# Fourier attention and gated MLP on one Trainium2 core: engine orders and PSUM banks from a list schedule of recorded instructions

## The chip, the core and the metric

The kernel runs on one core of one Trainium2 chip. The metric is device microseconds for one execution. Five engines have queues of their own and work strictly in the order of their queue: TensorE (PE in the rows; its weight loads are PEld), VectorE (DVE), ScalarE (ACT), GpSimd (POOL) and SyncE (SP, which here only issues DMAs). An engine waits for another at a semaphore, and everything behind the waiting instruction in its queue waits too.

## What is computed

Four batches of 1088 tokens with 128 features go through three stages, each in fp32:

```python
q_p, k_p = phi(q), phi(k)                  # products of two 8-wide projections, per head
x = (q_p @ kv) / (q_p @ z)                 # linear attention, kv = k_p^T v, z = sum of k_p
u = x + real(fft(fft(x, axis=1), axis=2))  # Fourier mixing over tokens and features
x2 = u + relu(norm(u) @ w_ch1) @ w_ch2     # channel MLP
h = relu(x2 @ w_in); gate, v = h[..., :512], h[..., 512:]
v_s = einsum('ts,bsd->btd', w_spatial, norm(v)) + b_spatial
out = (gate * v_s) @ w_out
```

The weights of the MLPs arrive as float64 and are turned into float32 on the chip. A wide fp32 product is made of fp32r products: each operand is split into a high and a low part, and three matmuls (high by high, high by low, low by high) are summed in PSUM.

## The kernel before, in words

Per batch there are four parts. **keys and queries** (`feats`, `keys`, `queries`): small matmuls into the tile `abp`, copied by ScalarE to `ab`, multiplied out by VectorE to `pp` (128x768); then `kv`, transposes `qps`, `nm`, and VectorE's division into `ub`. **Fourier** (`fourier_seq`, `fourier_feat`): VectorE folds `ub` (`eo`, `fe`, `l_`, `lrb`), TensorE makes `dft`, ScalarE copies it to `tb`, TensorE makes `ups` and `urm`, and VectorE adds them to `ub`. **channel**: statistics (`bst`, `mv`) and normalisation `un` of nine 128-token tiles, transposes `t1` and `t2`, then for each of three groups c of 384, 384 and 320 tokens the MLP in four blocks m: three matmuls into `h_`, ScalarE's relu `hh`, VectorE's remainder `hl`, three matmuls into `c2`. The sum goes to `xt` and is split into `xh` and `xl`; per 128 tokens `v_ps` is made, relu `v`, statistics, normalisation; and v is split into `vh` (ScalarE) and `vlo`. **spatial**: for each group c and each of four feature blocks m, 24 matmuls of `vh`, `vlo` with the spatial weights `wsh`, `wsl` and two for the remaining tokens and bias go into one accumulator `ac`; `u_ps` gives the gate, `uh` and `gl`/`gh` the gated product, `o` the output. Its matmuls of 384 or 320 columns are the bulk of TensorE's work: lines 608 to 610 have 1152 of them over the four batches.

There is one `vh`/`vlo` pair, so a batch's spatial part can begin only when its v is ready and the batch before is through with it. The spatial weights come in raw (`wst`, `w2st`) and are split too, in `spatial_split`: ScalarE makes `wsh`, VectorE or GpSimd `wsl`. The raw tiles of groups 0 and 1 share their buffers with `uh`, `gh`, `gl`, `sxh` and `sxl` of the spatial part (`ring`).

The order is set in three ways. The text of the kernel gives an order; the tile framework's scheduler may move instructions within it, by its own cost estimates; and some places are pinned by hand: `tc.keep_in_program_order` on the idle matmuls `wp` of `warm` and on `dft`, `tc.issue_after` on the first spatial weights. Batch b+1's `channel` and batch b's `spatial` are Python generators that the last loop (lines 640 to 654) advances by turns at the ratio `R`. Matmuls `wp` on zeros (`warm`, 11, 10 and 20 of them) are there to keep TensorE active. PSUM's eight banks are split between two pools, `psx` and `psy`, with fixed tags: `x` 3, `y` 1, `acc` 2, `us` 1, `o` 1.

Lines that the change touches: 195 (`un` on VectorE, a subtraction and a multiplication by per-partition scalars), 202 and 206, 271 (`vlo` of batch 0 on GpSimd, `sub(G, ...)`), the generators' `yield`s, `spatial` (588 to 638) and the loops behind 562.

Of the kernel before, what the change touches and what calls it, by code (L numbers as in the profile page):

```python
# [1 line left out]

# [5 lines left out]
F32 = mybir.dt.float32  # L8
# [55 lines left out]

@with_exitstack
def fourier_attention_gmlp_kernel(
# [18 lines left out]
    nc = tc.nc  # L85
    V, A, T, G = nc.vector, nc.scalar, nc.tensor, nc.gpsimd
# [23 lines left out]
    ub, x2, marks = {}, {}, {}  # L110
# [6 lines left out]
    def spatial_load(pool, c, stage):  # L117
# [47 lines left out]
    def channel(b, pe, psm, tagm, nm, psc, tagc, vn, hooks=(None,) * 7):  # L165
# [9 lines left out]
        def stats(tiles):  # L175
# [5 lines left out]
            r_ = rstd(pe, mv_, len(tiles), "l1", nb)  # L181
            for i, j in enumerate(tiles):
                mv[j], rs[j] = mv_[:, i, 0:1], r_[:, i, :]
# [6 lines left out]
        for c in range(3):  # L190
# [3 lines left out]
            for j, i in tiles:  # L194
                marks[b, c, "un"] = V.tensor_scalar(out=un[:, i, :], in0=u_[:, j, :], scalar1=mv[j], scalar2=rs[j],
                                op0=ALU.subtract, op1=ALU.mult)
            t1 = mt("t1")
            for j, i in tiles:
                marks[b, c, "t1"] = T.transpose(out=t1[:, 128 * i:128 * i + 128], in_=un[:, i, :], identity=ident if j < 8 else psel)
            unh = pe.tile([P, 384], F32R, tag="unh", bufs=nb, name="unh")  # L200
            unl = pe.tile([P, 384], F32R, tag="unl", bufs=nb, name="unl")
            marks[b, c, "unh"] = A.copy(out=unh[:, 0:n], in_=t1[:, 0:n])
# [6 lines left out]
            yield  # L209
# [32 lines left out]
            marks[b, c] = A.copy(out=xh[:, 0:n], in_=xt[:, 0:n])  # L242
# [8 lines left out]
            for j, i in tiles:  # L251
# [11 lines left out]
                yield  # L263
# [23 lines left out]
    sa = ExitStack()  # L287
    ca = sa.enter_context(tc.tile_pool(name="ca", bufs=1, side="right"))
    sp = ExitStack()
    pre = sp.enter_context(tc.tile_pool(name="pre", bufs=1, side="left"))  # L290
# [34 lines left out]
    def weight_load(tag, *blocks):  # L325
        t = const.tile([P, len(blocks), 512], I32, tag=tag, name="wraw")
        for i, (n, src, k) in enumerate(blocks):
            nc.sync.dma_start(out=t[:, i, :], in_=src.bitcast(I32)[:, 512 * k:512 * k + 512])
# [100 lines left out]
    def fourier_seq(b):  # L429
# [34 lines left out]
        def dft(par, sine, lhsT, rhs, last):  # L464
            c0 = 64 * (sine ^ par)
            m_ = mm(out=dps[par][c0:c0 + 64, 0:NCOL], lhsT=lhsT, rhs=rhs, start=(par, sine) not in done, stop=last,  # L466
                    tile_position=(0, c0))
            if done:
                tc.keep_in_program_order(m_)
# [50 lines left out]
    def warm(n):  # L520
        wp = psy.tile([P, 512], F32, tag="us", bufs=1, name="wp")
        for i in range(n):
            tc.keep_in_program_order(mm(out=wp, lhsT=wz[:, 0:128], rhs=wz, start=True, stop=True))
# [3 lines left out]
    nc.sync.dma_start(out=raw0, in_=sblk.bitcast(I32))  # L527
# [13 lines left out]
    nc.sync.dma_start(out=tr, in_=trig)  # L541
    nc.sync.dma_start(out=trr, in_=trig_r)
    nc.sync.dma_start(out=dd, in_=ddft)
# [18 lines left out]
    for _ in channel(0, pre, psy, "acc", 2, psy, "o", None, [convert(("w2", 0), ("w2", 1), ("wo", 0), ("wo", 1)), None, None, None, convert(("wi", 0), ("wi", 1)), None]):  # L562
        pass
# [3 lines left out]
    with tc.issue_after(marks[0, 1, "t1"].ins):  # L567
        spatial_split(pre, 0, [G], spatial_load(const, 0, ring))
# [186 lines left out]
```

## Time and profile before

| what | us |
|---|---|
| median of 3 runs | 455.65 (455.12 to 455.97) |
| span of the profiled execution, first to last instruction | 451.9 |
| median less that span | 3.75 |
| busy: TensorE, VectorE, ScalarE, GpSimd | 430.6, 276.3, 191.5, 67.1 |
| first matmul of the spatial part (`ac`) | at 73.30 |

The profiled execution has a span of its own and no separate time; the 3.75 us between it and the median lie before the first and behind the last instruction, or are the difference of the runs. Busy time is the union of an engine's instructions; a matmul overlaps the next one, so TensorE's pace is read from the distance of two starts, not from one matmul's length. Idle time of an engine is put down to the instruction of another engine that ended last before it went on.

### The profile page before, as it was taken

How to read it: one execution, taken by the hardware profiler on the slowest of the kernel's cores; microseconds unless marked ns; L12 is line 12 of the kernel's file. 1: busy time of each engine (PE TensorE's matmuls, PEld its weight loads, DVE VectorE, ACT ScalarE, POOL GpSimd, SP SyncE). 2: the span in 40 equal slices, each digit the busy share in tenths (PEclk: the TensorE clock that was granted, in tenths of full speed). 3: DMA queues.
4: the chain of work that ended last, by engine and by line, in shares of the span. 5: the costliest groups of instructions: out<-in, count | busy, mean ns of one | idle time of the engine just before them, and what ended most of it. 6: DMA issues, size and time to landing. Idle time of an engine off the chain costs nothing.

```text
span 451.9 us, 8066 instructions
## 1 busy us (share of the span) xinstructions
PE 430.6 (95%) x3181; PEld 392.3 (87%) x3181; DVE 276.3 (61%) x685; ACT 191.5 (42%) x448; POOL 67.1 (15%) x105
## 2 busy tenths in 40 slices
PE   8786999999999989999999999999999999999996
PEld 7555877768787878899999999999999999999995
DVE  5899898995657677788536454873727366221221
ACT  3755787455231345456424233552424255222211
POOL 2354684570111130000000000000000000000000
PEclk9999799999999999999999999999999999999998
DMA  8974151011004000000000000000000000000000
GB/s 256 363 249 159 36 167 48 1 47 27 1 1 133 19 0 0 1 20 1 16 0 1 17 1 1 19 15 1 1 1 17 1 18 1 16 0 19 0 19 15
DMA packets 13009, 19.32 MB, mean 43 GB/s; under 512 B 1446, under 2 KB 11436, under 8 KB 12844
## 3 DMA queue, kind: packets, MB, share of 16 engines
q1 hardware_dynamic: 12972, 18.82, 12.9%
q8 instruction: 25, 0.41, 0.4%
q14 instruction: 12, 0.10, 0.1%
HBM read 16.58 MB, written 2.23 MB: 42 GB/s over the span
## 4 chain that ended last, share of the span: by engine, by line
PE 73%; DVE 9%; issue 9%; ACT 4%; POOL 3%; DMA 1%; POOLq 0%; ACTq 0%; DVEq 0%
PE ac L610 12%; PE ac L608 12%; PE ac L609 12%; PE v_ps L254 2%; PE dft L466 2%; PE v_ps L256 2%; PE c L227 2%; PE c L225 2%; PE c L226 2%; PE v_ps L255 2%; PE ac L616 2%; PE ac L615 2%; PE u_ps L601 2%; PE u_ps L602 1%; PE u_ps L603 1%
## 5 line engine op out<-in xcount | busy, mean ns | idle before, releaser
L608 PE MATMUL ac<-wsh,vh 128*128 128x384 f32 (+1 forms) x384 | 126.6, 330 | 0.4 <-ACT vh L270 0.4
L610 PE MATMUL ac<-wsh,vlo 128*128 128x384 f32 (+1 forms) x384 | 126.4, 329 | 0.0
L609 PE MATMUL ac<-wsl,vh 128*128 128x384 f32 (+1 forms) x384 | 126.3, 329 | 0.0
L609 PEld LDWEIGHTS ac<-wsl,vh 128*128 128x128 f32 x384 | 72.1, 188 | 1.8 <-issue 0.8
L608 PEld LDWEIGHTS ac<-wsh,vh 128*128 128x128 f32 x384 | 72.1, 188 | 1.5 <-ACT vh L270 0.7
L610 PEld LDWEIGHTS ac<-wsh,vlo 128*128 128x128 f32 x384 | 72.1, 188 | 1.4 <-issue 0.6
L619 DVE TENSOR_TENSOR uh<-ac,uh 128x384 f32<-128x384 f32 (+1 forms) x48 | 25.5, 531 | 55.9 <-PE ac L616 55.2
L605 ACT ACTIVATE uh<-u_ps 128x384 f32<-128x384 f32 (+1 forms) x48 | 22.6, 471 | 48.0 <-PE u_ps L603 45.6
L114 DVE TENSOR_TENSOR gl<-uh,gh 128x384 fp32r<-128x384 f32 (+1 forms) x48 | 25.8, 538 | 13.5 <-ACT gh L620 13.4
L245 POOL CAST xh<-xh 128x64 fp32r<-128x64 f32 x4 | 2.0, 496 | 202.5 <-ACT xh L242 202.5
L361 DVE TENSOR_TENSOR pp<-ab 128x768 f32<-128x768 f32 x23 | 23.9, 1067 | 11.3 <-ACT ab L357 11.3
L620 ACT CAST gh<-uh 128x384 fp32r<-128x384 f32 (+1 forms) x48 | 23.6, 492 | 13.2 <-DVE uh L619 13.0
L261 DVE BATCH_NORM_STATS2 bst<-vn 128x6 f32<-128x512 f32 x27 | 18.6, 693 | 16.8 <-ACT vn L259 16.7
L259 ACT ACTIVATE vn<-v_ps 128x512 f32<-128x512 f32 x27 | 16.0, 598 | 19.2 <-PE v_ps L256 18.7
L241 DVE TENSOR_TENSOR xt<-c,xt 128x384 f32<-128x384 f32 (+1 forms) x12 | 6.4, 530 | 27.4 <-PE c L227 27.4
L227 PE MATMUL c<-hl,w 128*128 128x384 f32 (+1 forms) x48 | 16.7, 348 | 0.3 <-DVE hl L220 0.3
L282 ACT CAST vh<-vn 128x1024 fp32r<-128x1024 f32 x12 | 12.6, 1048 | 10.3 <-PE ac L609 8.1
L225 PE MATMUL c<-hh,w 128*128 128x384 f32 (+1 forms) x48 | 16.7, 348 | 0.0
L242 ACT CAST xh<-xt 128x384 fp32r<-128x384 f32 (+1 forms) x12 | 6.0, 496 | 25.0 <-DVE xt L241 24.9
L254 PE MATMUL v_ps<-wi,xh 128*128 128x512 f32 x36 | 15.5, 430 | 0.9 <-ACT v L259 0.8
L226 PE MATMUL c<-hh,w 128*128 128x384 f32 (+1 forms) x48 | 16.3, 340 | 0.0
L601 PE MATMUL u_ps<-sxh,wi 128*128 128x384 f32 (+1 forms) x48 | 16.3, 339 | 0.0
(714 smaller groups left out, 931.1 us busy)
## 6 DMA issues: line engine op xcount, KB each, us to landing
wst<-in_wsp SPq DMA_DIRECT2D x18, 192.0 KB, 4.0
vx<-in_vt SPq DMA_DIRECT2D x12, 198.0 KB, 4.0
kt<-in_kT SPq DMA_DIRECT2D x12, 192.0 KB, 3.6
qt<-in_qT SPq DMA_DIRECT2D x12, 192.0 KB, 4.5
w2st<-in_wsp SPq DMA_DIRECT2D x9, 160.0 KB, 5.6
tr<-in_trig SPq DMA_DIRECT2D x1, 1096.0 KB, 8.7
wraw<-in_w SPq DMA_DIRECT2D x4, 256.0 KB
wraw<-in_win SPq DMA_DIRECT2D x4, 256.0 KB, 6.2
```

The source lines that it names most:

```text
L114: eng.tensor_tensor(out=lo, in0=x, in1=hi.bitcast(F32), op=ALU.subtract)
L225: mm(out=c2[:, 0:n], lhsT=wpart("w2", 0, 128 * m, 128), rhs=hh[:, 0:n], start=(m == 0), stop=False)
L226: mm(out=c2[:, 0:n], lhsT=wpart("w2", 1, 128 * m, 128), rhs=hh[:, 0:n], start=False, stop=False)
L227: mm(out=c2[:, 0:n], lhsT=wpart("w2", 0, 128 * m, 128), rhs=hl[:, 0:n], start=False, stop=(m == 3))
L254: mm(out=h_, lhsT=xh[:, cs], rhs=wt["wi"][:, 2:4, 0, :], start=True, stop=False)
L361: (G if [b, tag[0], c] in [[3, 'k', 2]] else V).tensor_tensor(out=pp, in0=a_.unsqueeze(3).to_broadcast([P, 12, 8, 8]), in1=b_.unsqueeze(2) ...
L601: mm(out=h_[:, 0:n], lhsT=wpart("wi", 0, 128 * m, 128), rhs=xh[:, 0:n], start=True, stop=False)
L608: mm(out=ac[:, 0:n], lhsT=vh[:, k, ms], rhs=wsh[c][:, k, :], start=(k == 0), stop=False)
L609: mm(out=ac[:, 0:n], lhsT=vh[:, k, ms], rhs=wsl[c][:, k, :], start=False, stop=False)
L610: mm(out=ac[:, 0:n], lhsT=vl[:, k, ms], rhs=wsh[c][:, k, :], start=False, stop=False)
L619: V.tensor_tensor(out=uh[:, 0:n], in0=ac[:, 0:n], in1=uh[:, 0:n], op=ALU.mult)
L620: A.copy(out=gh[:, 0:n], in_=uh[:, 0:n])
```

## The change

The kernel no longer issues instructions as its text runs. Engines and tiles are stand-ins that record each instruction with what it reads and writes (`Plan`, `Op`, `Tile`, `View`). `price` gives each a duration by a formula. `arrange` runs a list schedule up to 12 times, alternately from the front and from the back, each time with urgencies from the last pass, and keeps the order with the least planned end; `run` then issues the instructions in that order under `tc.manual_schedule()`. PSUM has one pool of eight banks, and the schedule gives each tile a bank when its first instruction is placed. The hand-set order (`issue_after`, `keep_in_program_order`, the generators and `R`) is gone. DMAs are taken in the order of their recording as they become ready.

Two edits are in the arithmetic's place: `un` is made by ScalarE as Identity(scale * x + bias), with `sh` = -mean * rstd made by one VectorE instruction per batch; and batch 0's eight `vlo` are made by VectorE.

```diff
+class Plan:
...
+    def arrange(self):
+
+        self.edges()
+        best, urgent = None, [-r for r in self.rank]
+        for _ in range(self.rounds):
+            there = self.schedule(urgent, True)
+            if there is None:
+                break
+            ends, issued = there
+            if best is None or max(ends) < best[0]:
+                best = max(ends), issued, ends, {t: t.bank for t in self.banked}
+            back = self.schedule(ends, False)
+            if back is None:
+                break
+            urgent = [-e for e in back[0]]
...
+    def run(self):
+        self.arrange()
+        with self.tc.manual_schedule():
+            for o in self.issued:
+                o.emit()
...
+    def price(self, op):
...
+        elif e == "scalar":
+            op.busy = (160 if psum else 190) + n / 1.2
+        elif e == "vector":
+            if op.meth == "tensor_scalar" and not psum and not out.tile.pool.psum:
+                ptr = isinstance(kw.get("scalar1"), View)
+                op.busy, op.port = (260 if ptr else 145) + n / 1.92, True
...
+                        if s <= t:
+                            turn = e == "tensor" and mode is not None and o.mode != mode
+                            s = max(s, free[e] + 230 if turn else free[e], port if o.port and forth else 0.0)
+                            choice.append((sign * urgent[o.n] + (self.sticky if turn else 0.0), sign * o.n, s, o))
...
-    const = ctx.enter_context(tc.tile_pool(name="const", bufs=1, side="left"))
-    psx = ctx.enter_context(tc.tile_pool(name="psx", bufs=1, space=PSUM))
-    psy = ctx.enter_context(tc.tile_pool(name="psy", bufs=1, space=PSUM))
+    const = plan.pool("const", side="left")
+    psx = psy = plan.pool("ps", psum=True)
...
+            sh = pe.tile([P, len(tiles), 1], F32, tag="sh1", bufs=nb, name="sh")
+            V.scalar_tensor_tensor(out=sh, in0=mv_[:, :, 0:1], scalar=-1.0, in1=r_, op0=ALU.mult, op1=ALU.mult)
...
-                marks[b, c, "un"] = V.tensor_scalar(out=un[:, i, :], in0=u_[:, j, :], scalar1=mv[j], scalar2=rs[j],
-                                op0=ALU.subtract, op1=ALU.mult)
+                A.activation(out=un[:, i, :], in_=u_[:, j, :], func=ACTF.Identity, scale=rs[j], bias=mv[j])
...
-                        sub(G, vl[:, j, :], v_, vh[:, j, :])
+                        sub(V, vl[:, j, :], v_, vh[:, j, :])
...
-    with tc.issue_after(marks[0, 1, "t1"].ins):
-        spatial_split(pre, 0, [G], spatial_load(const, 0, ring))
+    spatial_split(pre, 0, [G], spatial_load(const, 0, ring))
...
     for b in range(B):
-        sg = spatial(b)
         if b + 1 < B:
-            R = [0.3, 2.2, 2.2][b]
...
+            channel(b + 1, pe, psx, "x", 3, psx, "y", vn)
+        spatial(b)
+    plan.run()
```

In the rows below `L168` is the line that issues everything in the new kernel. First, TensorE's queue around the first spatial matmul (`ac`). Before, with `c` the MLP's second product and `v_ps` the v of batch 0's last group still to come:

```order
L399 MATMUL qps<-prm,pp 128x128 x4
L227 MATMUL c_864<-hl,w_68 128x320
L399 MATMUL qps<-prm,pp 128x128 x2
L354 MATMUL abp<-sb_s,qt 64x2x32 x6
L608 MATMUL ac<-wsh_1199,vh 128x384
L609 MATMUL ac<-wsl_1200,vh 128x384
L610 MATMUL ac<-wsh_1199,vlo 128x384
L608 MATMUL ac<-wsh_1199,vh 128x384
L609 MATMUL ac<-wsl_1200,vh 128x384
L610 MATMUL ac<-wsh_1199,vlo 128x384
L254 MATMUL v_ps<-wi,xh 128x512
```

And in the new order, where the number in `kvz_73` and `kvz_65` tells odd and even batches apart:

```order
L168 MATMUL c_1342<-hh,w_1055 128x320 x2
L168 MATMUL nm<-kvz_65,qp 64x66 x7
L168 MATMUL v_ps<-wi,xl 128x512 x3
L168 MATMUL c_1342<-hl,w_1055 128x320
L168 MATMUL nm<-kvz_65,qp 64x66 x12
L168 MATMUL nm<-kvz_73,qp 64x66 x12
L168 MATMUL ac<-wsh_1463,vh 128x384 x4
L168 MATMUL ac<-wsl_1471,vh 128x384
L168 MATMUL ac<-wsh_1463,vlo 128x384
```

The first `ac` now stands behind all `v_ps` of batch 0's second group, as before, and also behind the `abp`, `kv` and most `nm` of all four batches; four accumulators are opened at once instead of one.

Second, VectorE's queue at the Fourier fold of batch 0 (`eo`, `fe`, `l_`, `lrb` are its steps, `pp` belongs to the keys and queries of batch 1). Before:

```order
L312 TENSOR_SCALAR dy<-wraw 128x256
L442 TENSOR_TENSOR eo<-ub 128x512 x2
L446 TENSOR_TENSOR fe<-eo 128x4x63
L455 TENSOR_TENSOR lrb<-rs__414 32x63
L451 TENSOR_TENSOR l__416<-fe 128x2x64 x2
L455 TENSOR_TENSOR lrb<-rs__414 32x63
L446 TENSOR_TENSOR fe<-eo 128x4x63
L455 TENSOR_TENSOR lrb<-rs__414 32x63
L451 TENSOR_TENSOR l__416<-fe 128x2x63 x2
L455 TENSOR_TENSOR lrb<-rs__414 32x63
```

And now:

```order
L168 TENSOR_TENSOR eo<-ub 128x512 x2
L168 TENSOR_TENSOR pp<-ab 128x768 x4
L168 TENSOR_TENSOR fe<-eo 128x4x63
L168 TENSOR_TENSOR l__79<-fe 128x2x63
L168 TENSOR_TENSOR pp<-ab 128x768 x2
L168 TENSOR_TENSOR fe<-eo 128x4x63
L168 TENSOR_TENSOR l__79<-fe 128x2x63
L168 TENSOR_TENSOR lrb<-rs__421 32x63 x4
```

The six `pp` of batch 1 stand between the steps of batch 0's fold where there were none.

Third, VectorE's queue in the MLP of batch 1 (`hl` is the remainder of a block m, `unl` that of the normalised input). Before, these are the first group's four blocks:

```order
L114 TENSOR_TENSOR unl<-t_1972,unh 128x384
L195 TENSOR_SCALAR un<-ub,mv_1933,r_1961 128x128 x2
L220 SCALAR_TENSOR_TENSOR hl<-h__2268,hh 128x384
L220 SCALAR_TENSOR_TENSOR hl<-h__2276,hh 128x384
L220 SCALAR_TENSOR_TENSOR hl<-h__2284,hh 128x384
L220 SCALAR_TENSOR_TENSOR hl<-h__2298,hh 128x384
L241 TENSOR_TENSOR xt<-c_2267,xt 128x384
L619 TENSOR_TENSOR uh<-ac,uh 128x384
```

And now the end of the second group's four blocks, `hl<-h__2339` being the last of them:

```order
L168 SCALAR_TENSOR_TENSOR hl<-h__2297,hh 128x384
L168 TENSOR_TENSOR xl<-xt,xh 128x384
L168 SCALAR_TENSOR_TENSOR hl<-h__2303,hh 128x384
L168 SCALAR_TENSOR_TENSOR hl<-h__2309,hh 128x384
L168 BN_STATS bst<-vn 128x6
L168 BN_AGGR mv_2351<-bst 128x2
L168 BN_STATS bst<-vn 128x6
L168 SCALAR_TENSOR_TENSOR hl<-h__2339,hh 128x384
```

The `un` between them are gone from VectorE, and everything of keys, queries and Fourier for all batches stands ahead of both pieces, in both orders.

## Rows read from the trace of the kernel before

**Rows 1.** The page: span, and busy time of the engines.
```profile
span 451.9 us, 8066 instructions
...
PE 430.6 (95%) x3181; PEld 392.3 (87%) x3181; DVE 276.3 (61%) x685; ACT 191.5 (42%) x448; POOL 67.1 (15%) x105
```

**Rows 2.** Windows: length; busy us of PE, PEld, DVE, ACT, POOL; granted clock; DMA.
```profile
0.00:73.00 73.00, 61.09 (x583) 48.67 (x585) 61.83 (x165) 45.73 (x115) 37.48 (x54) 0.95 0.60 195
73.00:171.00 98.00, 92.91 (x961) 76.76 (x958) 69.94 (x163) 40.34 (x99) 27.40 (x45) 1.00 0.10 29
0.00:171.00 171.00, 154.00 (x1538) 125.43 (x1539) 131.77 (x327) 86.07 (x213) 64.88 (x99) 0.98 0.31 100
40.00:60.00 20.00, 16.97 (x103) 14.31 (x103) 17.58 (x39) 14.94 (x37) 12.69 (x13) 0.83 0.35 108
...
60.00:100.00 40.00, 37.43 (x336) 29.15 (x338) 36.28 (x80) 24.83 (x57) 25.52 (x30) 1.00 0.20 57
200.00:440.00 240.00, 240.00 (x1438) 234.37 (x1437) 120.54 (x295) 89.19 (x199) 1.48 (x4) 1.00 0.03 9
```

**Rows 3.** Waits of VectorE from 73 to 171 us: total us, times, longest.
```profile
DVE ub L503 <- PE ups L495: 7.7, 4, 4.4
DVE pp L361 <- ACT ab L357: 7.5, 7, 2.1
DVE rd L420 <- PE nm L411: 3.7, 2, 1.8
```

**Rows 4.** TensorE in order of time: start, length, line, tiles, the idle time before.
```profile
73.30 0.44 PE L608 MATMUL ac<-wsh,vh 128*128 128x384 f32 x1
73.58 0.34 PE L609 MATMUL ac<-wsl,vh 128*128 128x384 f32 x1
73.76 0.34 PE L610 MATMUL ac<-wsh,vlo 128*128 128x384 f32 x1
...
171.51 0.34 PE L225 MATMUL c<-hh,w 128*128 128x384 f32 x1
```

**Rows 5.** The same view of TensorE at 40 to 46 us.
```profile
40.59 0.33 PE L199 MATMUL t<-prm,un 128*128 128x128 f32 x1 [1.95 <-DVE un L195]
...
43.74 0.69 PE L216 MATMUL h__641<-unl,w 128*128 128x384 f32 x1 [0.81 <-DVE unl L114]
44.23 0.52 PE L214 MATMUL h__649<-unh,w 128*128 128x384 f32 x1
44.55 0.52 PE L215 MATMUL h__649<-unh,w 128*128 128x384 f32 x1
```

**Rows 6.** VectorE by line and shape: count, busy us, mean ns, idle before.
```profile
L195 DVE TENSOR_SCALAR un<-ub,mv,r 128x128 f32<-128x128 f32 x36 | 11.4, 360 | 0.1
...
L114 DVE TENSOR_TENSOR vlo<-vn,vh 128x1024 fp32r<-128x1024 f32 x12 | 14.6, 1214 | 0.3 <-ACT vh L282 0.3
...
L261 DVE BATCH_NORM_STATS2 bst<-vn 128x6 f32<-128x512 f32 x27 | 18.6, 693 | 16.8 <-ACT vn L259 16.7
...
L114 DVE TENSOR_TENSOR xl<-xt,xh 128x384 fp32r<-128x384 f32 x8 | 4.8, 595 | 1.8 <-ACT xh L242 1.5
...
L114 DVE TENSOR_TENSOR wsl<-wst,wsh 128x384 fp32r<-128x384 f32 x4 | 5.2, 1367 | 0.0
...
L220 DVE SCALAR_TENSOR_TENSOR hl<-h__2268,hh 128x384 fp32r<-128x384 f32 x1 | 0.6, 558 | 2.2 <-ACT hh L219 2.2
```

**Rows 7.** GpSimd by line and shape.
```profile
L114 POOL TENSOR_TENSOR wsl<-wst,wsh 128x384 fp32r<-128x384 f32 x12 | 15.5, 1314 | 1.9 <-ACT wsh L134 1.7
L114 POOL TENSOR_TENSOR vlo<-v,vh 128x512 fp32r<-128x512 f32 x8 | 10.8, 1378 | 6.0 <-ACT vh L270 6.0
```

**Rows 8.** ScalarE by line and shape.
```profile
L314 ACT ACTIVATE dy<-dy,cst 128x256 int32<-128x256 int32 x10 | 5.1, 506 | 0.1
...
L311 ACT ACTIVATE dr<-wraw 128x256 f32<-128x256 uint32 x10 | 4.4, 443 | 4.4 <-POOL w L114 2.5 <-POOL wo L114 1.5 <-POOL wi L114 0.2
...
L277 ACT CAST a<-vn 128x128 fp32r<-128x128 f32 x12 | 3.5, 294 | 0.0
```

More of the change, by code (lines that the diff above doesn't have):

```diff
@@ new lines, with __init__, tile, open @@
+class Pool:
+    def __init__(self, plan, name, after=None, psum=False, **kw):
+        self.plan, self.name, self.prev, self.kw, self.psum = plan, name, after, kw, psum
+        self.tiles, self.tags, self.stack, self.handle = [], {}, None, None
+    def tile(self, shape, dtype, tag=None, bufs=1, name=None):
+        t = Tile(self, shape, dtype, tag or name, bufs, name)
+        if not self.psum:
+            self.tags.setdefault(t.tag, []).append(t)
+        self.tiles.append(t)
+        if self.psum:
+            self.plan.banked.append(t)
+        return t
+    def open(self):
+        if self.handle is None:
+            if self.prev is not None:
+                self.prev.stack.close()
+                self.plan.opened.remove(self.prev)
+            self.stack = ExitStack()
+            kw = dict(space=PSUM) if self.psum else self.kw
+            self.plan.opened.append(self)
+            self.handle = self.stack.enter_context(self.plan.tc.tile_pool(name=self.name, bufs=1, **kw))
+        return self.handle
@@ new lines, with emit, __init__, __getattr__ @@
+class Op:
+    __slots__ = ("n", "eng", "meth", "args", "kw", "pre", "busy", "lag", "mode", "port", "banked", "start", "end")
+    def emit(self):
+        if self.eng.handle is not None:
+            r = lambda v: v.real() if isinstance(v, View) else v
+            getattr(self.eng.handle, self.meth)(*[r(v) for v in self.args], **{k: r(v) for k, v in self.kw.items()})
+class Engine:
+    def __init__(self, plan, name, handle):
+        self.plan, self.name, self.handle = plan, name, handle
+    def __getattr__(self, meth):
+        def record(*args, **kw):
+            return self.plan.add(self, meth, args, kw)
+        return record
@@ L284, in conv @@
         conv_rem(ms, vn[:, 8, ms])
[L287 to L290, printed above, removed]
+    ca = plan.pool("ca", side="right")
+    pre = plan.pool("pre", side="left")
     tr = ca.tile([P, 2, 4, NCOL], F32, name="tr")
@@ L465, in dft @@
             c0 = 64 * (sine ^ par)
-            m_ = mm(out=dps[par][c0:c0 + 64, 0:NCOL], lhsT=lhsT, rhs=rhs, start=(par, sine) not in done, stop=last,
+            mm(out=dps[par][c0:c0 + 64, 0:NCOL], lhsT=lhsT, rhs=rhs, start=(par, sine) not in done, stop=last,
                     tile_position=(0, c0))
-            if done:
-                tc.keep_in_program_order(m_)
             done[par, sine] = True
@@ L566, in fourier_attention_gmlp_kernel @@
     loads(2)
[L567 to L571 removed]
+    spatial_split(pre, 0, [G], spatial_load(const, 0, ring))
+    pw = plan.pool("pw", after=pre, side="left", reuse_waits="tile")
     spatial_split(ca, 1, (V, G), spatial_load(pw, 1, ring))
@@ L580, in fourier_attention_gmlp_kernel @@
         fourier_feat(b)
-    sa.close()
-    pe = ctx.enter_context(tc.tile_pool(name="pe", bufs=1, side="right", reuse_waits="tile"))
+    pe = plan.pool("pe", after=ca, side="right", reuse_waits="tile")
     w2st = pe.tile([P, 10, CH[2][1]], F32, tag="vn", name="w2st")
@@ L589, in spatial @@
     def spatial(b):
-        pend = None
         for c in range(3):
```

350 lines of the change are left out of this document (296 added, 54 removed).

## The prediction

> **What bounds the kernel now.** I read the page first: TensorE is busy 430.6 of 451.9 us, VectorE 276.3 [rows 1]. A share of 95% says little about where time is to be had, so I went to the windows. From 200 to 440 us TensorE is busy 240.00 of 240.00 us at granted clock 1.00 [rows 2]; a matmul of 384 columns starts 0.18 us after the one before it (73.58 to 73.76) [rows 4], and no order makes that shorter. The reader is to see there that the last 280 us are TensorE at its own pace. The time to be had lies before. Of the first 171 us TensorE is idle 17.0 (171 less 154.0), and VectorE is idle 39.2: 11.2 of the first 73 us, 28.1 of the 98 behind [rows 2].
>
> The waits of VectorE say what the 28.1 are. Between 73 and 171 us it waits 7.7 us for `ups`, 7.5 for `ab` and 3.7 for `nm` [rows 3], 18.9 in all: keys, queries and Fourier of batches 1 to 3, which TensorE's queue hands out in small portions between `ac` matmuls. Nothing there is short of work; the two engines take turns.
>
> **The mark.** To compare the orders I choose a place from which TensorE has the same work left in both. Before, it is the matmul at 171.51 us [rows 4]: behind it stand 926 matmuls of 384 columns, 584 of 320, 81 of 512 and 48 of 128. In the new order, behind the third block's `c2<-hl` of batch 1's second group stand 937, 584, 75 and 42: eleven at 0.18 us more, six wider and six narrower ones less, equal to within half a us. The matmul there needs `hl`, and the last `hl` of that group (`h__2339`, the third place shown above) stands close behind, so I take that as VectorE's mark. Whatever the new order gains by the mark it keeps, as TensorE is full behind it, and the tail (last `o`, copy, DMA) is the same. So the question is one number: when is the new order at the mark?
>
> **VectorE's work ahead of the mark.** By 171 us it has been busy 131.8 us [rows 2]. The new order puts the same front work ahead of the mark, with these differences, counted over both orders:
> - `un`: 15 gone, at 0.360 us [rows 6]: -5.4.
> - `vlo` of batch 0: 8 more. VectorE has no such row. A subtraction of 1024 columns takes 1.214 and one of 384 takes 0.595 [rows 6]; on the line between them 512 columns take 0.72: +5.8. The lower end is 0.595 each (+4.8), the upper 1.367, which is what `wsl` takes on VectorE while GpSimd does its share of the same split (+10.9).
> - `hl`: 4 more at 0.558: +2.2; `bst` of v: 2 more at 0.693: +1.4 [rows 6].
> - `unl`, `xl`, `xt` one more each and `uh`, `gl` one less each, all of about 0.56: +0.6. Two `sh` and one `mv`, which are among the smallest instructions: I put +0.6 for them.
>
> Sum: +5.2, so 137.0 us of busy time.
>
> **Its idle time.** This is what the change is about, and no row shows it. Ends: the 11.2 of the first 73 us hold the wait for the first loads, which stays; if the order takes out 3 of them and no idle time is added, 8. At the other end, from 60 to 100 us, where VectorE is the fuller engine, it idles 3.7 of 40 [rows 2], that is 0.09 per us; over the some 75 us that remain that gives 7, and twice that, 14, added to 8 gives 22. I take 11.2 plus half of 7, 15 in round: the keys and queries now stand early (TensorE has all `abp` and `kv` ahead of the first `ac`, the first place shown above), and the second place shows `pp` filling the gaps of batch 0's fold. So the mark is at 137.0 + 15 = 152.0 instead of 171.5: **19.5 us less**.
>
> Can TensorE be there by then? Until 171 us it is busy 154.0 [rows 2]. In that are some 24 matmuls that follow at 0.32 us (44.23 to 44.55 [rows 5]) instead of 0.18, 3.4 us, after TensorE had waited for `unl` and before that for `un`; without them it is 150.6, and that still contains the stretched steps within it. So it allows 152 but not much less unless those steps shrink too, which is a second reason for not taking 8.
>
> **What costs nothing.** `un` on ScalarE: a copy of 128 columns is 0.294 us; two activations of 256 columns with and without a pointer bias are 0.506 and 0.443 [rows 8], so a pointer costs 0.06 and `un` with two about 0.42. 15 of them ahead of the mark are 6.3 us beside 86.1 of busy time until 171 [rows 2]: 92 of 152, so VectorE and TensorE hide it. Were ScalarE full, three `un` in a row before `t1` would be 1.3 us per batch, and `hh`, queued behind them, would wait with `hl` and `c2` behind it. GpSimd loses eight `vlo` of 1.378, 11.0 us [rows 7]; I count nothing for that but a little in the lower end below. SyncE: the first spatial weights no longer wait for `t1`; they go out right behind the loads of batch 2, ahead of those of batch 3, so they should land no later than now.
>
> **A rule against the change.** `wsl` on VectorE takes 1.367 beside GpSimd, a subtraction of the same shape 0.595 alone [rows 6]; GpSimd's own takes 1.314 [rows 7]. In the new order GpSimd's eight `wsl` of group 0 fall into the stretch of the first `vlo`, so part of the eight could take 1.37 each: 5.2 us on the sum. The Trainium skill (SBUF — State Buffer, "Who interferes with whom") says that a VectorE instruction with two SBUF inputs and a GpSimd instruction that reads SBUF exclude each other, the later one waiting for the whole of the other. By that rule, every `vlo` waiting out a `wsl`, the sum would be 8 x 1.31 = 10.5 us worse; the trace agrees with the doubling but shows no wait that long on each. I leave it out of the sum, since the eight `vlo` taken off GpSimd remove as many meetings, and put it among the rivals.
>
> **The numbers.** The profiled execution would come to 451.9 - 19.5 = 432.4 us; the median lies 3.75 above the span, so 436.2. With idle time 8 the gain is 26.5 and the time 429.2, and some 3 us less where GpSimd no longer holds VectorE up: 426. With 22 it is 12.5: 443.2.
>
> **Rivals.**
> - *Lock.* All eight `vlo` meet `wsl`: 5.2 more, 441.4, or 448.4 with idle time 22. For it: rows 6 and 7. Against: only part of them can coincide. 0.09.
> - *Half the idle time stays.* Engines work in queue order, the plan's durations are formulas (`un` 0.30 instead of 0.42), and one late instruction holds all behind it. VectorE's idle time is then 25 to 33: 446 to 454. For it: 18.9 us of its waits were of this kind [rows 3]. 0.12.
> - *Slower, by TensorE's clock.* From 40 to 60 us the granted clock is 0.83 [rows 2], part of it at 1.2 GHz, after TensorE had been kept waiting [rows 5]. The new order spends its last idle matmuls `wp` just ahead of batch 0's first `t1`, and some 90 us of work by the paces stand between there and the mark. A us of work at 1.2 GHz costs one more. TensorE's work ahead of the mark is about 137 by counts and paces, so 15 of 152 are slack; from some 35 us of work at the low level on the gain is used up, and with 45, half of it, the time is 436 + 30 = 466. Against: TensorE idles before the mark now too, and behind 60 us every window shown is at 1.00. The Trainium skill (TensorE: Matmul & The Clock Gate, "HAM oscillation — how this bites in real kernels") warns that a matmul stream interrupted by waits again and again falls back to half clock each time; no row here shows that repeating. 0.07.
> - *Nothing happens*, because the built program keeps an order of its own or TensorE's stretched steps move with the order: 455. The order shown speaks against it. 0.02.
>
> The forecast has 0.70. Time 436.2. A measurement of this kernel can tell about 0.2% from no change, some 0.9 us. Forecast, lock and half case are all faster: 0.91; same 0.02; slower 0.07. The range 425 to 449 takes in the forecast's ends, the lock and the nearer part of the half case; the clock, nothing, the far part of the half case and a better result than 425 are left out, under 0.2 together.
>
> **What would show it.** Right: VectorE idle 8 to 22 us before the last `hl` of batch 1's second group, at 145 to 159 us; the first `ac` some us later than 73.30 (more `pp` stand ahead of it on VectorE) but with all `kv` done; granted clock 1.00 from there; TensorE full behind 160. Wrong: VectorE waiting for `hh`, `ab` or `ups` in the same amounts as in rows 3; `vlo` at 1.3 us; a window at 0.8 or less behind 50 us; or a gap of TensorE behind the mark, where I expect none.

## The result and the profile after

The changed kernel takes 434.67 us (median of 4 runs, 433.52 to 436.83), the kernel before 455.53 beside it: a ratio of 0.9552, interval 0.9522 to 0.9582. Its profiled execution took 434.07 us with a span of 432.3; 436.2 and 432.4 were forecast. That the total is so near is in part luck: it hides errors that cancel, which the readings below show.

First the page's busy times and slices of the changed kernel, to be held against [rows 1]:

```profile
span 432.3 us, 8148 instructions
PE 422.8 (98%) x3181; PEld 391.7 (91%) x3181; DVE 265.9 (62%) x661; ACT 205.1 (47%) x484; POOL 55.0 (13%) x97
PEclk9999999999999999999999999999999999999999
```

VectorE has 24 instructions fewer (36 `un` gone, eight `vlo` and four `sh` come), ScalarE 36 more, GpSimd eight fewer, and in this execution the granted clock never leaves its upper level. The windows (us of the stretch, then busy time and count of PE, PEld, DVE, ACT and POOL, granted clock, DMA share, GB/s) answer to [rows 2]:

```profile
0.00:73.00 73.00, 69.00 (x977) 57.38 (x978) 59.34 (x152) 46.61 (x125) 20.83 (x41) 1.00 0.54 182
40.00:60.00 20.00, 19.57 (x261) 15.80 (x258) 16.21 (x54) 14.96 (x41) 7.38 (x9) 1.00 0.14 47
60.00:100.00 40.00, 37.91 (x337) 33.15 (x334) 37.84 (x85) 29.07 (x69) 16.40 (x24) 1.00 0.14 38
0.00:156.80 156.80, 150.41 (x1541) 124.30 (x1542) 130.99 (x330) 95.65 (x238) 53.28 (x91) 1.00 0.33 109
```

By 73 us TensorE has been busy 69.0 us where it was 61.1. This is where the mark stands, the third block's `c<-hl` of batch 1's second group on TensorE, behind the last `hl` of the group on VectorE; the first `ac` is shown ahead of them:

```profile
81.03 0.97 PE L168 MATMUL ac<-wsh,vh 128*128 128x384 f32 x4
156.36 0.54 DVE L168 SCALAR_TENSOR_TENSOR hl<-h__2339,hh 128x384 fp32r<-128x384 f32 x1
157.00 0.34 PE L168 MATMUL c<-hl,w 128*128 128x384 f32 x1
```

The mark is reached at 157.00. For a mark that can be set in every order alike I count TensorE's work back from the last matmul, at the pace of matmuls that follow each other without a wait (0.175 us for 384 columns, 0.147 for 320, 0.233 for 512, 0.109 for 128), and take the place that has 272.0 us left. That is 171.7 us before and 156.8 after. So 14.9 us of the 19.6 in the span were won ahead of the mark, and 4.7 behind it: from the mark to the end it is 280.2 us before, 275.5 after. The prediction had 19.5 and none.

Here are the windows of the kernel before up to its mark, and from 40 to 50 us:

```profile
0.00:171.70 171.70, 154.70 (x1542) 126.13 (x1543) 131.77 (x327) 86.07 (x213) 64.88 (x99) 0.98 0.31 99
40.00:50.00 10.00, 7.75 (x28) 6.96 (x29) 8.32 (x24) 5.85 (x14) 3.40 (x5) 0.66 0.41 134
```

Ahead of the mark TensorE's idle time fell from 17.0 to 6.4 us, and its busy time for the same work from 154.7 to 150.4. Most of the second is the clock: a granted clock of 0.66 means 6.8 of 10 us at the lower level, 1.2 GHz, where work takes twice as long, so some 3.4 us of the gain are a stretch at half clock that the new order does not have.

What is behind the mark can be seen in part in the waits of TensorE (waiting tile, releaser, us in total, times, longest), from 171 us on, of the kernel before:

```profile
PE o__4965 L626 <- ACT gh L620: 1.1, 1, 1.1
```

The same view of the changed kernel from 157 us on is empty: the list puts matmuls of the last group where the old order waited for the last `gh`. The other 3.6 us are scattered, at most 0.8 in ten us, and no row names a cause. They are lost ahead of the last matmul, which starts 3.6 us before the end in the one kernel and 3.5 in the other:

```profile
448.32 0.42 PE L628 MATMUL o__4965<-gl,wo 128*128 128x320 f32 x1
```

```profile
428.83 0.38 PE L168 MATMUL o__5076<-gl,wo 128*128 128x320 f32 x1
```

VectorE's waits between 73 and 157 us, against [rows 3]:

```profile
DVE ub L168 <- PE ups L168: 5.4, 2, 4.2
DVE hl L168 <- ACT hh L168: 1.8, 2, 1.3
DVE bst L168 <- ACT v L168: 1.1, 1, 1.1
```

The waits for `ab` and `nm` are gone from this stretch, and that for `ups` has shrunk from 7.7 to 5.4 us. What is left of the first two stands in the first 73 us:

```profile
DVE pp L168 <- ACT ab L168: 4.3, 4, 3.1
DVE rd L168 <- PE nm L168: 2.9, 2, 2.3
```

In all VectorE idles 25.8 us ahead of the mark (156.8 less 130.99); before it was 39.9 (171.7 less 131.77). The moved instructions, each line busy us and mean ns:

```profile
L168 DVE TENSOR_TENSOR vlo<-v,vh 128x512 fp32r<-128x512 f32 x8 | 5.5, 697 | 0.0
L168 DVE TENSOR_TENSOR wsl<-wst,wsh 128x384 fp32r<-128x384 f32 x4 | 2.3, 614 | 0.0
L168 ACT ACTIVATE un<-ub,sh,r 128x128 f32<-128x128 f32 x36 | 15.6, 488 | 0.0
L168 POOL TENSOR_TENSOR wsl<-wst,wsh 128x384 fp32r<-128x384 f32 x12 | 12.3, 1051 | 6.8 <-ACT wsh L168 6.7
```

`vlo` takes 0.70 us on VectorE (0.72 had been taken); `wsl` on VectorE is down from 1.367 to 0.614, on GpSimd from 1.314 to 1.05; `un` takes 0.488 on ScalarE, not 0.42.

### The profile page after: what moved, and what is told of

Same layout as the page of the kernel before. It is cut to its first block, busy times and chain, and to the rows that moved or that the text cites. A ratio compares the mean times of both kernels' runs of the same rounds, so it can differ in the third digit from the quotient of the medians.

```text
span 432.3 us, 8148 instructions
## 1 busy us (share of the span) xinstructions
PE 422.8 (98%) x3181; PEld 391.7 (91%) x3181; DVE 265.9 (62%) x661; ACT 205.1 (47%) x484; POOL 55.0 (13%) x97
## 4 chain that ended last, share of the span: by engine, by line
PE 83%; DVE 10%; DMA 3%; ACT 2%; issue 1%; ACTq 0%
PE ac L168 44%; PE u_ps L168 6%; PE v_ps L168 5%; PE c L168 4%; PE dft L168 3%; PE wp L168 3%; PE t L168 2%; DMA qt<-in_qT 2%; PE abp L168 1%; PE kv L168 1%; PE ups L168 1%; PE nm L168 1%; DMA vx<-in_vt 1%; PE qps L168 1%; DVE ub L168 1%
## 5 line engine op out<-in xcount | busy, mean ns | idle before, releaser
L168 PE MATMUL ac<-wsh,vh 128*128 128x384 f32 (+1 forms) x384 | 102.0, 329 | 1.6 <-ACT vh L168 1.6
L168 PE MATMUL ac<-wsh,vlo 128*128 128x384 f32 (+1 forms) x384 | 102.5, 329 | 0.0
L168 PE MATMUL ac<-wsl,vh 128*128 128x384 f32 (+1 forms) x384 | 102.1, 330 | 0.1
L168 DVE TENSOR_TENSOR uh<-ac,uh 128x384 f32<-128x384 f32 (+1 forms) x48 | 25.6, 533 | 80.2 <-PE ac L168 71.8
L168 PEld LDWEIGHTS ac<-wsh,vh 128*128 128x128 f32 x384 | 68.3, 188 | 3.1 <-ACT vh L168 2.2
L168 PEld LDWEIGHTS ac<-wsh,vlo 128*128 128x128 f32 x384 | 68.2, 188 | 1.0
L168 PEld LDWEIGHTS ac<-wsl,vh 128*128 128x128 f32 x384 | 68.2, 188 | 1.0 <-POOL wsl L168 0.4
L168 ACT ACTIVATE uh<-u_ps 128x384 f32<-128x384 f32 (+1 forms) x48 | 22.6, 474 | 69.4 <-PE u_ps L168 68.5
L168 ACT CAST gh<-uh 128x384 fp32r<-128x384 f32 (+1 forms) x48 | 23.7, 494 | 22.1 <-DVE uh L168 18.3
L168 DVE TENSOR_TENSOR gl<-uh,gh 128x384 fp32r<-128x384 f32 (+1 forms) x48 | 25.3, 535 | 9.9 <-ACT gh L168 7.3
L168 PE MATMUL u_ps<-sxh,wi 128*128 128x384 f32 (+1 forms) x96 | 29.4, 331 | 0.4 <-DVE ub L168 0.4
L168 PE MATMUL ac<-wr,a 128*128 128x384 f32 (+1 forms) x96 | 29.7, 329 | 0.0
L168 PE MATMUL c<-hh,w 128*128 128x384 f32 (+1 forms) x96 | 28.5, 331 | 0.0
L168 DVE TENSOR_TENSOR pp<-ab 128x768 f32<-128x768 f32 x23 | 22.5, 1013 | 5.9 <-ACT ab L168 4.3
L168 POOL CAST xh<-xh 128x64 fp32r<-128x64 f32 x4 | 1.2, 304 | 195.6 <-ACT xh L168 195.6
L168 DVE BATCH_NORM_STATS2 bst<-vn 128x6 f32<-128x512 f32 x27 | 18.3, 688 | 11.6 <-ACT vn L168 11.5
L168 PE MATMUL v_ps<-wi,xh 128*128 128x512 f32 x72 | 23.3, 398 | 0.0
L168 ACT ACTIVATE vn<-v_ps 128x512 f32<-128x512 f32 x27 | 15.6, 599 | 12.2 <-PE v_ps L168 12.0
L168 PEld LDWEIGHTS u_ps<-sxh,wi 128*128 128x128 f32 x96 | 17.7, 188 | 1.3 <-DVE ub L168 0.8
L168 DVE TENSOR_TENSOR vlo<-vn,vh 128x1024 fp32r<-128x1024 f32 x12 | 14.6, 1220 | 5.9 <-ACT vh L168 5.8
L168 PEld LDWEIGHTS c<-hh,w 128*128 128x128 f32 x96 | 17.5, 188 | 0.8 <-ACT hh L168 0.2
L168 PEld LDWEIGHTS ac<-wr,a 128*128 128x128 f32 x96 | 17.8, 188 | 0.2
```

The costliest lines, as they stand in the source:

```text
L168: getattr(self.eng.handle, self.meth)(*[r(v) for v in self.args], **{k: r(v) for k, v in self.kw.items()})
```

## The experiments

My theory (A): the order sets the time, by how long VectorE and TensorE wait for each other ahead of the mark. Rivals: the two arithmetic edits do it (B), the clock (C), GpSimd's hold on VectorE (L), the free choice of PSUM banks. "Planned anew" means that the list was run again for the edited kernel, so that its order differs too; "in place" means that the changed kernel's order and banks were kept. The ratios are to the kernel before, timed beside each (454.5 to 455.5 us). The columns: median, ratio with its interval, the mark as counted above, VectorE's busy and idle time ahead of it and the granted clock there.

| kernel | us | ratio (interval) | mark | VectorE busy, idle | clock |
|---|---|---|---|---|---|
| before | 455.53 | 1 | 171.7 | 131.8, 39.9 | 0.98 |
| changed | 434.67 | 0.9552 (0.9522 to 0.9582) | 156.8 | 131.0, 25.8 | 1.00 |
| 1 both edits undone, planned anew | 446.49 | 0.9828 (0.9772 to 0.9883) | 169.3 | 139.5, 29.8 | 0.97 |
| 2 `vlo` back, planned anew | 447.88 | 0.9851 (0.9815 to 0.9887) | 171.4 | 136.5, 34.9 | 0.96 |
| 3 `un` back, planned anew | 441.59 | 0.9720 (0.9686 to 0.9755) | 161.3 | 139.7, 21.6 | 0.99 |
| 4 old order, both edits | 462.48 | 1.0160 (1.0131 to 1.0190) | 178.3 | 130.4, 47.9 | 0.95 |
| 5 `vlo` back in place | 436.36 | 0.9602 (0.9566 to 0.9638) | 158.5 | 132.4, 26.1 | 1.00 |
| 6 old banks, planned anew | 448.76 | 0.9878 (0.9838 to 0.9918) | 170.5 | 136.5, 34.0 | 0.98 |
| 7 no idle matmuls, planned anew | 439.03 | 0.9648 (0.9614 to 0.9681) | 159.8 | 130.9, 28.9 | 0.96 |
| 8 turns free, planned anew | 438.34 | 0.9641 (0.9614 to 0.9668) | 160.6 | 134.6, 26.0 | 1.00 |
| 9 both edits undone in place | 437.70 | 0.9624 (0.9591 to 0.9656) | 160.4 | 136.5, 23.9 | 1.00 |
| 10 prices from the trace | 438.32 | 0.9623 (0.9598 to 0.9648) | 161.1 | 137.7, 23.4 | 0.99 |
| 11 best | 431.09 | 0.9477 (0.9452 to 0.9502) | 152.9 | 132.2, 20.7 | 1.00 |
| 12 no idle matmuls, in place | 432.72 | 0.9524 (0.9501 to 0.9548) | 155.3 | 130.3, 25.0 | 0.99 |

In every list-made order the span less the mark is 275.4 to 276.1 us; in the two with the old order (before, 4) 280.2 and 280.9. So the 4.7 us behind the mark come with the list's order or with its way of issuing, which no run separates (run 6 has the old banks and does not lose them), and what else differs between the kernels lies ahead of it.

**1, 2, 3: edits undone one by one, the list run again.** 1 and 2:

```diff
-                        sub(V, vl[:, j, :], v_, vh[:, j, :])
+                        sub(G, vl[:, j, :], v_, vh[:, j, :])
```

1 and 3:

```diff
-                A.activation(out=un[:, i, :], in_=u_[:, j, :], func=ACTF.Identity, scale=rs[j], bias=mv[j])
+                V.tensor_scalar(out=un[:, i, :], in0=u_[:, j, :], scalar1=mv[j], scalar2=rs[j], op0=ALU.subtract, op1=ALU.mult)
```

In 1 and 3 `sh` is gone too, and `mv[j]` is the mean again.

> The list schedule and the free choice of banks stay, both arithmetic edits are undone: low part of v of batch 0 on GpSimd again, first normalisation (un) on VectorE again. Theory A (the order decides: it cuts the time that VectorE and TensorE spend waiting for each other ahead of 157 us): VectorE's work ahead of the mark changes by 15 x 0.36 - 8 x 0.69 = -0.1 us, so 434.7, between 432 and 438. Theory B (the arithmetic edits decide, because GpSimd no longer holds VectorE up and ScalarE shortens the way to t1): half or more of the 20.9 us goes, 445 or more. Theory C (only the stretch of matmuls at half clock at 42 to 50 us, 3.4 us, and the last stall went with the order): 450.

> Only the low part of v of batch 0 goes back to GpSimd. Theory A in its strict form (VectorE's busy time plus a fixed idle time is the time to the mark): 8 x 0.69 = 5.5 us less VectorE work ahead of the mark, so 429 to 431. Theory B (a subtraction on GpSimd holds up VectorE and comes late for the ac matmuls): 437 to 442. If VectorE's work is not what sets the time: 434.7 within 1.

> Only the first normalisation goes back to VectorE (15 x 0.36 us ahead of the mark). Theory A, strict: 434.7 + 5.4 = 440. If waits between engines and not VectorE's work set the time: within 2 us of 434.7, or less, as un takes 0.49 us on ScalarE and 0.36 on VectorE and stands in the chain from the statistics to t1.

Measured 446.49, 447.88 and 441.59. The first lies where B had put it, the third near the 440 of strict A, the second where no theory had it. A in its strict form falls with the second: 5.5 us of work taken off VectorE made the kernel 13 us slower. A place in the first kernel shows one way in which GpSimd comes in (timeline: start, us, engine, instruction, idle time before and releaser):

```profile
120.96 4.14 DVE L168 TENSOR_TENSOR lrb<-rs__1823 32x63 f32<-32x63 f32 x2
121.04 0.19 POOL L168 TENSOR_TENSOR lz<-eo 128x2 f32<-128x2 f32 x1
121.19 1.93 POOL L168 TENSOR_TENSOR wsl<-wst,wsh 128x384 fp32r<-128x384 f32 x2
123.09 0.71 POOL L168 TENSOR_TENSOR wi<-dr,wi 128x256 fp32r<-128x256 f32 x1
123.77 1.25 POOL L168 TENSOR_TENSOR vlo<-v,vh 128x512 fp32r<-128x512 f32 x1
125.92 0.73 PE L168 MATMUL dft<-tr,l__1814 128*64 128x274 f32 x2 [3.27 <-DVE ub L168]
```

A two-input VectorE instruction of 32x63 elements, 0.22 us at the median, stands for 3.93 us (its maximum in the tile's view) and ends when GpSimd's unbroken row of four subtractions does. TensorE then waits 3.27 us, and the window from 120 to 140 us has a granted clock of 0.91. In the second kernel TensorE waits 4.5 us ahead of a `nm` and 4.3 ahead of a `dft`, both times for VectorE's `ub`. But three kernels that differ in order as well as in engines can't tell whether GpSimd or the new order costs the 13 us. The fifth run does.

**4: the edits alone in the old order.** The changed kernel's two edits in the old kernel, with `sh` added.

> The old kernel with its own order, with the two arithmetic edits alone. Theory A (the order decides): 455.5 within 3 us. Theory B (the edits decide): 445 or less. GpSimd's eight low parts of 1.38 us come off, so the meetings with VectorE in batch 0's channel part are rarer: A would allow 1 to 2 us for that.

It is slower by 1.6%, against B, and worse than A's "no change". The waits of TensorE up to 180 us:

```profile
PE t L200 <- ACT un L197: 4.5, 2, 2.7
PE h__897 L215 <- ACT xt L209: 1.8, 1, 1.8
PE c L228 <- DVE hl L221: 1.3, 1, 1.3
```

The wait for `un` has grown from 3.9 to 4.5 us with the engine changed, and three `vlo` (from 65.95 us) stand on VectorE ahead of the `unl` for which TensorE then waits 0.67 us; the window from 60 to 80 us has clock 0.83. In the old order the edits cost time.

**5 and 9: the changed kernel's order kept, the engines changed at the time of issue.**

```diff
+            gp = next(o.eng for o in self.ops if o.eng.name == "gpsimd")
             for o in self.issued:
+                if o.eng.name == "vector" and o.kw.get("out") is not None:
+                    if o.kw["out"].tile.name == "vlo" and o.kw["out"].idx.size == 512:
+                        o.eng = gp
                 o.emit()
```

9 also issues each `un` as the old subtraction and product on VectorE; the four `sh` stay.

> The changed kernel's order and banks are kept as they are; only the eight low parts of v of batch 0 are handed to GpSimd at the same places of the order. Theory L (lock: VectorE's instructions with two inputs in SBUF stand still while GpSimd subtracts, for a whole run of GpSimd's instructions, as the 3.93 us of one 32x63 subtraction at 121 us of the first experiment's kernel): VectorE gets 5.5 us of work less ahead of the mark, but 5 us or more of stretched instructions and, with TensorE kept waiting, half clock: 440 to 447. Theory P (the list schedule happened to find a poorer order when vlo was on GpSimd): 434.7 within 3 us, as the order is the same.

> The changed kernel's order and banks are kept; both arithmetic edits are undone in place: the eight low parts of v of batch 0 on GpSimd, the first normalisation (un) on VectorE at the places where ScalarE had it. Theory order and banks (the edits are worth little by themselves; the fifth run's 1.7 us for the low parts, and un's 5.4 us of VectorE work, part of which lands in its idle time): 436 to 441. Theory edits (the order is good only because the edits take the load off VectorE): 445 or more, as in the first experiment.

436.36 and 437.70. The windows up to each kernel's mark, of 5:

```profile
0.00:158.50 158.50, 149.84 (x1542) 124.51 (x1543) 132.36 (x323) 95.95 (x238) 64.48 (x99) 1.00 0.33 107
```

and of 9:

```profile
0.00:160.40 160.40, 151.19 (x1542) 125.08 (x1543) 136.51 (x341) 89.17 (x220) 64.81 (x99) 1.00 0.33 106
```

In 5 the eight `vlo` (5.5 us) have left VectorE, and its busy time is 1.4 us *more*: there is one more `uh` ahead of the mark (0.5 us), and its other instructions are stretched by some 6 us while GpSimd works. So L is real in VectorE's busy time, but in time it is worth at most some 1.7 us here, which is not clear of the noise (the intervals of 5 and of the changed kernel overlap). In 9 `un` brings 4.2 us of VectorE work, 2.2 of which fall into idle time, and the mark is 1.9 us later. With both edits undone the order and its banks alone give 437.70: 17.8 of the 20.9 us; the edits are worth the other 3.0. The 17.8 stand for the new order, its banks and its way of issuing (`manual_schedule`) together: no run issues the old order in the new way. And 1 and 9 do the same arithmetic on the same engines, but for the four `sh`; the 8.8 us between them are the order and its banks alone. So B is out, though run 1 had looked like it.

**6: the old banks.** In the list, and likewise where it takes a bank:

```diff
+        fixed = dict(x=(0, 1, 2), y=(3,), us=(4,), acc=(5, 6), o=(7,))
...
-                    if not banks or t.long and lasting >= 5 or len(banks) < 2 and t.outer[not forth] & ~done:
+                    own = fixed[t.tag]
+                    free_ = [x for x in banks if x[1] in own]
+                    if not free_ or len(own) > 1 and len(free_) < 2 and t.outer[not forth] & ~done:
                         return None
```

> Both arithmetic edits and the list schedule stay, but a PSUM tile may only take the banks that its tag had before (three for x, one each for y, us and o, two for acc). Theory banks (free choice of banks lets the front's tiles run ahead): 442 to 450, with TensorE's waits ahead of the mark back at 12 us or more. Theory order alone: 434.7 to 438.

448.76: 14 of the 21 us are gone, and the mark is at 170.5, near the old 171.7. Waits of TensorE in this kernel up to 180 us:

```profile
PE dft L168 <- DVE l__860 L168: 2.8, 1, 2.8
PE qps L168 <- DVE pp L168: 2.1, 2, 1.4
PE qps L168 <- ACT qp L168: 1.9, 4, 0.6
```

The third row is the bank itself: `qps` waits four times until ScalarE has copied an earlier one out of its bank; the changed kernel has no such wait. The windows from 80 to 120 us, of this kernel and then of the changed one, show the stretch with its longest waits:

```profile
80.00:120.00 40.00, 32.13 (x273) 22.83 (x272) 37.88 (x93) 17.98 (x42) 17.77 (x32) 0.91 0.16 46
```

```profile
80.00:120.00 40.00, 38.04 (x290) 30.95 (x287) 37.33 (x89) 16.67 (x37) 17.55 (x28) 1.00 0.16 46
```

VectorE is as full in both; in the one TensorE has work meanwhile, in the other it waits and loses clock. The Trainium skill (Perfetto Trace Analysis, "Optimization Strategy") says that a gap which repeats on the engine that should be full can mean too little PSUM for the next tile; this trace agrees, with up to 0.6 us, four times. What stays open is how much of the 14 us is banks: the order was made anew with them, and planning anew alone has moved the time by up to 11.5 us (run 2 against run 5, the same work on the same engines). Only the 1.9 us of waits for a bank are read from the trace.

**7 and 12: the idle matmuls.** 7 leaves out `warm(10)` and `warm(20)` and plans anew; 12 keeps the order and skips the last 30 `wp` at issue.

> The 30 idle matmuls of batch 0 (10 and 20) are gone, the first 11 stay. Theory clock (the idle matmuls keep TensorE at the upper level in the front): windows at 0.9 or less ahead of 100 us and 438 to 445. Theory VectorE (it and its waits set the time to the mark; TensorE has slack there): 434.7 within 2. Theory TensorE (the front is full): 30 x 0.22 = 6.5 us less, 428.

> The changed kernel's order and banks are kept; only the last 30 of the 41 idle matmuls are not issued (they compute nothing that is used). Theory clock (without them TensorE waits unbroken in the front and falls to the lower level): a window at 0.9 or less ahead of 100 us, mean clock under 0.99, and 437 to 442. Theory filler (the idle matmuls stand where TensorE would wait anyway, and no order was disturbed): clock 1.00 and 432 to 435. Theory queue (they stand in front of work that is ready): up to 6 us less, 429 to 432.

439.03 and 432.72. The matmuls left out compute nothing that is used. 7 looks like theory C:

```profile
50.00:60.00 10.00, 6.45 (x31) 5.66 (x31) 8.53 (x19) 8.86 (x25) 4.99 (x7) 0.83 0.01 2
80.00:90.00 10.00, 5.99 (x50) 3.91 (x46) 9.72 (x23) 5.81 (x13) 5.91 (x7) 0.76 0.14 41
```

12 says otherwise:

```profile
20.00:30.00 10.00, 8.93 (x164) 8.13 (x164) 8.40 (x18) 3.84 (x12) 1.50 (x8) 0.83 1.01 336
80.00:90.00 10.00, 8.93 (x48) 8.03 (x47) 9.72 (x23) 7.02 (x16) 8.59 (x10) 1.00 0.36 102
```

One fall at 20 to 30 us, none in the windows up to 160 us behind it, and no loss (its interval overlaps the changed kernel's). In 7 the clock fell also where its own new order made TensorE wait: its longest waits, 2.6 us for `ab` and 2.0 for `xl`, stand at 50 and 84 us, at those two windows. So without these idle matmuls nothing is lost as long as the order stays; what 7 lost came with its order.

**8 and 10: other rules for the list.** 8 sets `sticky`, what the list adds against a turn of TensorE between two kinds of matmuls, to 0; 10 drops the list's rule that VectorE and GpSimd exclude each other and sets the prices to the trace's durations, for `un` and the other pointer activations for example:

```diff
+            if op.kw.get("func") != ACTF.Relu and isinstance(kw.get("bias"), View):
+                op.busy += 190 if isinstance(kw.get("scale"), View) else 100
```

> The list schedule no longer holds back a turn of TensorE between its two kinds of matmuls (sticky 2500 to 0); the rest stays. Theory turns (a turn costs 0.1 to 0.2 us and the list saves them): 3 to 6 us more, 438 to 441, with more turns ahead of the mark. Theory lock and waits: any list order with the two arithmetic edits gives nearly the same, 433 to 438.

> Only the list's prices change, to the durations of the trace: un 0.49 us on ScalarE instead of 0.30, the first eleven idle matmuls 0.43 instead of 0.22, small and strided VectorE instructions 0.06 to 0.19 more, GpSimd 0.05 to 0.07 more, and no rule that VectorE and GpSimd exclude each other. Theory prices (an order is as good as the durations it was made with): 430 to 433. Theory chance (orders of like quality differ by some us in either direction, as with the turn rule of the eighth run): 434.7 within 4.

438.34 and 438.32. In 8 TensorE changes 106 times ahead of the mark between matmuls with 128 columns of weights (`128*128` in the rows) and narrower ones (`128*64`, `128*32`), against 56 in the changed kernel. Its busy time up to the mark is 156.6 us against 150.4, its idle time 4.0 against 6.4. So 50 turns more stand beside 6.2 us more of busy time, 0.12 us each, which is in the range expected; the 3.7 us of time are less than planning anew can do by itself. In 10 better prices gave a worse order: theory chance. How far chance reaches, three pairs of runs with the same work on the same engines show: planned anew they are 6.3 (7 against 12), 8.8 (1 against 9) and 11.5 us (2 against 5) slower than in the changed kernel's order. All three are slower, so the changed kernel's order may itself be a good draw. Below 11.5 us no time of a run that was planned anew tells a cause by itself.

**11: a better version.** The prices of 10, batch 0's second normalisation on ScalarE too, two more `pp` on GpSimd, and 80 rounds with small random changes of urgency, every sixth of them from the best so far, of which the best is kept:

```diff
-    def __init__(self, tc, lasting=(), rounds=12, sticky=2500.0):
+    def __init__(self, tc, lasting=(), rounds=80, sticky=2500.0):
...
             urgent = [-e for e in back[0]]
+            if i >= 8:
+                urgent = [u + rng.normal() * 200.0 for u in urgent]
...
-        (G if [b, tag[0], c] in [[3, 'k', 2]] else V).tensor_tensor(
+        (G if [b, tag[0], c] in [[3, 'k', 2], [2, 'k', 2], [1, 'k', 2]] else V).tensor_tensor(
...
-                V.tensor_scalar(out=v_, in0=v_, scalar1=mv2[:, i, 0:1], scalar2=rs2[:, i, :],
-                                op0=ALU.subtract, op1=ALU.mult)
+                if vn is None:
+                    A.activation(out=v_, in_=v_, func=ACTF.Identity, scale=rs2[:, i, :], bias=sh2[:, i, :])
...
```

(`vn is None` means batch 0; code between the pieces is left out; `sh2` is made as `sh` is.)

> The prices of the tenth run, the second normalisation of batch 0 on ScalarE too (9 x 0.54 us less on VectorE), two more products pp of keys (batches 1 and 2, third chunk) on GpSimd (2 x 1.0 less on VectorE, 2 x 1.5 more on GpSimd), and 80 rounds of the list with small changes of urgency instead of 12. Theory VectorE and its waits set the front: 7 us less work ahead of the mark and a better order, 424 to 430. Theory TensorE is at its limit there: 432 to 435. Theory contention (GpSimd's products hold VectorE up as long as they spare it): 430 to 434.

431.09, ratio 0.9477 (0.9452 to 0.9502), below the changed kernel's interval. Its window up to the mark:

```profile
0.00:152.90 152.90, 147.72 (x1541) 123.93 (x1542) 132.19 (x324) 101.53 (x248) 61.22 (x93) 1.00 0.35 111
```

VectorE is busy as long as in the changed kernel although some 7 us were taken off it; what fell is its idle time, to 20.7 us. Others of its instructions are longer: the eight `vlo` now take 0.882 us each where they took 0.697, with GpSimd busy 61.2 us up to the mark instead of 53.3.

```profile
L168 DVE TENSOR_TENSOR vlo<-v,vh 128x512 fp32r<-128x512 f32 x8 | 7.1, 882 | 0.7 <-ACT vh L168 0.7
```

That fits the contention theory (430 to 434); as the order was planned anew, how much each of the edits brought stays open.

## Why the prediction came out right, and what in it was wrong

- **The time and the place: right.** 434.67 lies in the range, near 436.2. The front was where time was to be had, VectorE's idle time there fell, from 39.9 to 25.8 us, and no window of the profiled execution is under 1.00. TensorE's busy time up to the mark is 150.4, where 150.6 was worked out without the stretch at 0.32 us. The first `ac` came at 81.03, with the last `kv` at 59.8, as the signs had it. That the sum comes so close to the measured span (432.4 and 432.3) is luck, as the next points show.
- **"Whatever the new order gains by the mark it keeps, as TensorE is full behind it": wrong by 4.7 us.** Busy for 240.00 of 240.00 us [rows 2] is not at full pace: ends of matmuls are modelled, and each overlaps the next, so small waits don't show as idle time. From the mark to the start of the last matmul it is 276.6 us before for 271.9 of work by paces (and 272.0 after), which would have shown it, from counts that the prediction had. 1.1 of the 4.7 is the wait for the last `gh`; the cause of the rest is open.
- **The idle time: wrong.** 15 was taken, 8 to 22 allowed; it is 25.8, 13.7 in the first 73 us (none of the 11.2 was taken out, as keys and queries were only moved there) and 12.1 behind. The latter is 0.14 per us; the rate of 0.09 came from a stretch where VectorE is nearly full, which says little about the others.
- **The work: wrong the other way.** 137.0 was taken, it is 131.0. `un` is near (4.2 us by runs 5 and 9, -5.4 in the sum). `vlo` was put at +5.8 with the lock left out, "since the eight `vlo` taken off GpSimd remove as many meetings". Run 5 shows that the lock left out was not nothing: with the eight back on GpSimd VectorE's other work is some 6 us longer, so the relief is as large as the 5.5 us that they take. So the mark came at 156.8 instead of 152.0, and the two errors ahead of it (+10.8, -6.0) and the one behind (-4.7) cancel.
- **From span to median: mis-sized.** 3.75 us was added. In every execution of this record that has both numbers the time lies 1.7 to 1.9 us above its span (434.07 and 432.3 here), so the profiled execution of the kernel before was some 2 us faster than its median. Without that the sum would have been near 434.2.
- **`un` on ScalarE: mis-sized, without effect.** 0.42 was taken, 0.488 measured. The Trainium skill (ScalarE: Activation LUTs, "What ACT_TABLE_LOAD costs") gives 186 ns, 0.833 ns per element and 93 ns for each pointer, by estimate 0.479 us for 128 columns with two; the trace agrees.
- **The rivals.** Lock: it did not come, `vlo` takes 0.70. Half the idle time: 25.8 lies outside the forecast's 8 to 22 and at this rival's lower end, so it was nearer than its 0.12; its time, 446 to 454, did not come because the work was 6.0 us less. The clock: it did not fall here, and the 3.4 us that it cost before are part of the gain; in runs 1, 2, 4 and 7 it is 0.95 to 0.97 over the front, each time with a TensorE that had waited.
- **Not seen at all: the banks.** The prediction spoke of the order alone. In run 6 two thirds of the gain are gone with the old banks, but its order is another too, so the banks' share is not shown. Run 4 shows that the edits by themselves make the kernel 1.6% slower, which the prediction had not asked either.

## What to carry to other kernels

Count the work by pace from the end back to a common place, not by busy share: it separates what an order wins in the front from what it loses in stalls too short to be idle time. Before judging an edit inside a scheduled kernel, make it in place, with the order held: planned anew, the same edits moved this kernel by 6 to 12 us for reasons that were not their own. And where engines take turns through PSUM, ask first whether a tile waits for a bank that only its tag may use.

## What was not expected of the hardware

A two-input VectorE instruction of 32x63 elements stood 3.93 us (run 1), through a whole row of four GpSimd subtractions and not one of them. The Trainium skill (SBUF — State Buffer, "Who interferes with whom") speaks of one instruction that blocks the other for its length; this run shows more than that. Taking eight subtractions of 0.70 us off VectorE left it busier by 1.4 us, 0.5 of which is one more `uh` (run 5). And 30 idle matmuls taken out of a fixed order cost nothing: one window of 10 us is at 0.83, and the span is 1.5 us shorter (run 12).
